# Two small products on opposite halves of TensorE's rows

## The chip, the cores and the metric

The kernel runs on one core of one Trainium2 chip. The metric is the device time of one execution in microseconds (us), the lower the better. The granted clock of TensorE was between 0.997 and 1.000.

## The reference, cut to what matters

```python
# q, k, v: (8 batches, 8 heads, 576 tokens, 64)
q_s = softmax(q, axis=-1)                      # over the 64 of a token
k_s = softmax(k, axis=2)                       # over the tokens
kv  = einsum('bhsd,bhse->bhde', k_s, v)        # K^T V: 64 x 64 for each head
x   = einsum('bhsd,bhde->bhse', q_s, kv)       # x: 576 x 64 for each head
# heads side by side: x is 4608 x 512
out = (silu(x @ w_gate) * (x @ w_val)) @ w_out # widths 512 -> 1536 -> 512
```

Most of the work is the feed-forward part in the last line. This case is about the two einsums, "kv" and "x".

## The kernel before

TensorE is an array of 128 x 128. Both einsums use it as four tiles of 64 x 64: the upper and the lower half of the rows (the contraction), times the left and the right half of the columns (the output partitions). `HALF[0]` and `HALF[1]` are the two halves of the partitions. In kv the row half is `g`, in x it is the head `h`; the other letter is the column half.

```python
    def kv_mm(b, G, kv, c):
        ek = st[b, G]["ek"]
        for t in range(T):                      # T = 9
            for g in range(2):                  # row half
                for h in range(2):              # column half
                    nc.tensor.matmul(
                        out=kv[g][HALF[h], c:c + 65], lhsT=ek[HALF[g], t, h, :],
                        rhs=vbs[G][HALF[g], t, h, :],
                        start=(t == 0), stop=(t == T - 1),
                    )

    def x_and_next_kv(b, with_kv=True):
        # ... 8 PSUM banks: main (4), kv (2), tail (2)
        def quads(o, c, G, t0, t1):
            for g in range(2):                  # column half
                for h in range(2):              # row half
                    nc.tensor.matmul(
                        out=o[h][HALF[g], c:c + 64 * (t1 - t0)], lhsT=kn[HALF[h], g, G, :],
                        rhs=qt[G][HALF[h], t0:t1, 64 * g:64 * g + 64],
                        start=True, stop=True,
                    )

        for G in range(NG):                     # NG = 2 groups of four heads
            quads(main[G], 0, G, 0, 8)          # x of batch b: 4 matmuls of 512 columns
            if more:
                kv_mm(b + 1, G, kv, 256 * G)    # kv of batch b + 1: 36 of 65 columns
        for G in range(NG):
            quads(tail, 64 * G, G, 8, T)        # x, last 64 columns
        # ... ScalarE and VectorE copy the banks out
```

I call one run of the two last loops a block. Every matmul is preceded by a load of its stationary operand (`lhsT`, 64 columns). The feed-forward matmuls `g_ps`, `u_ps`, `o_ps` (128 x 128, up to 512 columns) fill the time between the blocks; the prediction's "m unit" is one pair of `g_ps` and `u_ps` with the work of ScalarE and VectorE (`hr`) on it, and a bank is one of the buffers in PSUM that the matmuls write. Five blocks have x and kv together: x of batches 2 to 6.

The softmax here doesn't subtract the row's maximum and nothing guards it: scores larger than these inputs give would overflow.

## Time and profile before

| | before |
|---|---|
| median of 3 runs | 311.7 us (311.62 to 311.92) |
| span of the profiled run | 309.7 us |
| TensorE busy / VectorE / ScalarE | 302.8 / 161.9 / 146.3 us |
| one block, first x matmul to next g_ps | 1.298 us |
| five blocks | 6.5 us, 2.1% of the time |

How to read it: only TensorE counts, and of TensorE's time the change touches a fiftieth. The profile's lines for this, the waits and the timeline of a block are shown in the prediction. A timeline merges equal instructions; the trace also holds each instruction's start on its own, in whole nanoseconds. Where I give starts in ns they are such single records, counted from the first matmul of the block of batch 3. Matmul ends are modelled by the profile. The starts hardly vary: the five blocks of the kernel before took 1.297 or 1.298 us each.

### The profile page before, as it was taken

Reading aid. Unit: us, or ns where it says so; the run is one execution under the profiler, and the core shown is the slowest. Engines: PE = TensorE matmul, PEld = TensorE weight load, DVE = VectorE, ACT = ScalarE, POOL = GpSimd, SP = SyncE. Lnnn points to the kernel's source line nnn. Section 1 sums busy time; section 2 is a strip of 40 time slices with the busy share of each in tenths; the row PEclk is TensorE's granted clock in tenths of the full one; section 3 lists DMA queues with packets and bytes.
Section 4 is the critical chain, followed back from the end, with each engine's and each line's share of the span. In section 5 each row is a group of like instructions: output and inputs, shape, how many; then the busy total and the mean of one; then the engine's idle time right before and its main releaser. Section 6 shows DMA issues by size and latency. Waiting matters only on the chain.

```text
span 309.7 us, 5467 instructions
## 1 busy us (share of the span) xinstructions
PE 302.8 (98%) x2182; PEld 150.3 (49%) x2182; DVE 161.9 (52%) x286; ACT 146.3 (47%) x214; POOL 32.8 (11%) x39
## 2 busy tenths in 40 slices
PE   6999999999999999999999999999999999999995
PEld 2688745554445444454445444544444444444443
DVE  3844477945754566365826492639353324433421
ACT  5843578785674375547464737455043113312300
POOL 2960021510200110002000200000000000000000
PEclk9999999999999999999999999999999999999999
DMA  7999999999347815590739352605310302020133
GB/s 273 189 195 207 275 389 389 349 219 389 79 87 200 327 33 114 135 382 13 144 74 353 102 121 61 186 0 107 72 35 0 70 11 56 3 68 8 26 71 103
DMA packets 43018, 45.78 MB, mean 148 GB/s; under 512 B 19568, under 2 KB 28272, under 8 KB 42992
## 3 DMA queue, kind: packets, MB, share of 16 engines
q1 hardware_dynamic: 34096, 39.95, 43.4%
q0 software_dynamic: 8752, 5.31, 12.0%
q8 instruction: 17, 0.28, 0.4%
q10 hardware_dynamic: 144, 0.16, 0.2%
q14 instruction: 9, 0.07, 0.1%
HBM read 37.75 MB, written 9.44 MB: 152 GB/s over the span
## 4 chain that ended last, share of the span: by engine, by line
PE 96%; DMA 1%; DVE 0%; ACT 0%; issue 0%
PE g_ps L284 30%; PE u_ps L284 30%; PE o_ps L317 29%; PE kv L189 2%; PE xp L245 1%; PE idle L388 1%; DMA q<-in_q_dram 1%; PE tp L164 1%; PE o_ps L338 1%; DVE rs L135 0%; PE xp L202 0%; PE kv L411 0%; ACT eq L121 0%; ACT xt L259 0%; PE ks L397 0%; DVE o_sb L342 0%
## 5 line engine op out<-in xcount | busy, mean ns | idle before, releaser
L291 ACT ACTIVATE sg<-g_ps 128x512 bf16<-128x512 f32 (+2 forms) x120 | 64.7, 554 | 133.6 <-PE g_ps L284 120.5
L293 DVE TENSOR_TENSOR hr<-sg,u_ps 128x512 bf16<-128x512 bf16 (+3 forms) x120 | 72.5, 616 | 86.3 <-PE u_ps L284 80.7
L284 PE MATMUL g_ps<-xt,wg 128*128 128x512 bf16 (+2 forms) x480 | 111.4, 358 | 0.1
L284 PE MATMUL u_ps<-xt,wv 128*128 128x512 bf16 (+2 forms) x480 | 111.3, 358 | 0.0
L317 PE MATMUL o_ps<-wo,hr 128*128 128x512 bf16 x420 | 93.9, 379 | 0.0
L284 PEld LDWEIGHTS <-wv 128*128 128x128 bf16 x480 | 46.9, 98 | 46.4
L284 PEld LDWEIGHTS <-wg 128*128 128x128 bf16 x480 | 46.3, 98 | 45.5 <-issue 0.6
L317 PEld LDWEIGHTS <-hr 128*128 128x128 bf16 x420 | 40.9, 98 | 48.6
L110 DVE COPY o_sb<-o_ps 128x512 f32<-128x512 f32 x33 | 22.4, 680 | 39.0 <-PE o_ps L317 39.0
L124 POOL CAST vb<-v 128x1152 bf16<-128x1152 f32 x14 | 17.8, 1277 | 135.8 <-DMA v<-in_v_dram 106.6
L135 DVE TENSOR_REDUCE rs<-eq 128x18 f32<-128x1152 bf16 (+2 forms) x18 | 21.7, 1213 | 12.7 <-ACT eq L121 12.7
L149 DVE TENSOR_TENSOR qs<-eq,rr 128x1152 bf16<-128x1152 bf16 (+2 forms) x18 | 22.1, 1234 | 0.1
L121 ACT ACTIVATE eq<-q 128x1152 bf16<-128x1152 f32 (+2 forms) x18 | 18.3, 1051 | 4.1 <-DMA q<-in_q_dram 4.0
L121 ACT ACTIVATE ek<-k 128x1152 bf16<-128x1152 f32 (+2 forms) x17 | 17.9, 1101 | 0.5 <-DMA k<-in_k_dram 0.5
L291 ACT ACT_TABLE_LOAD x12 | 15.4, 1283 | 0.2
L121 ACT ACT_TABLE_LOAD x11 | 14.1, 1283 | 0.2
L388 PE MATMUL idle<-zero 128*128 128x512 bf16 x20 | 7.9, 560 | 2.6 <-DVE rs L135 1.4
L259 ACT CAST xt<-xp 128x512 bf16<-128x512 f32 x14 | 7.8, 586 | 4.5 <-PE xp L245 4.5
L260 DVE CAST xt<-xp 128x512 bf16<-128x512 f32 x14 | 9.0, 683 | 0.7 <-PE xp L245 0.7
L189 PEld LDWEIGHTS <-ek 64*64 64x64 bf16 x504 | 6.3, 107 | 1.7 <-ACT qt L108 0.4
L189 PE MATMUL kv<-vb,ek 64*64 64x65 bf16 x504 | 6.7, 194 | 0.0
L245 PE MATMUL xp<-qt,kn 64*64 64x512 bf16 (+1 forms) x112 | 6.7, 292 | 0.0
(44 smaller groups left out, 67.4 us busy)
## 6 DMA issues: line engine op xcount, KB each, us to landing
q<-in_q_dram SPq DMA_DIRECT2D x16, 576.0 KB, 5.4
out_dram<-o_sb SPq DMA_DIRECT2D x70, 128.0 KB, 2.3
k<-in_k_dram SPq DMA_DIRECT2D x12, 576.0 KB, 7.2
v<-in_v_dram SPq DMA_DIRECT2D x12, 576.0 KB, 9.1
wo<-in_moe_w_out_dram POOLq DMA_DIRECT2D x4, 384.0 KB, 15.4
k<-in_k_dram SPq DMA_DIRECT2D x4, 320.0 KB, 8.2
k<-in_k_dram SPq DMA_DIRECT2D x4, 256.0 KB, 8.1
v<-in_v_dram SPq DMA_DIRECT2D x2, 320.0 KB, 6.9
```

Source lines behind the costliest of these rows:

```text
L110: eng.tensor_copy(out=out, in_=in_)
L121: nc.scalar.activation(out=e[:, t0:t1], in_=src[:, t0:t1], func=AF.Exp)
L124: return nc.gpsimd.tensor_copy(out=vbs[G][:, :, :, 0:64], in_=raw["v", b, G].rearrange("p h (t d) -> p t h d", d=64),)
L135: i = nc.vector.reduce_sum(out=rs[:, 2 * t0:2 * t1], in_=eq2[:, 2 * t0:2 * t1, :], axis=mybir.AxisListType.X)
L149: last = eng.tensor_mul(qs[:, t0:t1, :].rearrange("p t (h d) -> p (t h) d", d=64), eq2[:, 2 * t0:2 * t1, :], s["rr"][:, 2 * t0:2 * t1].to_ ...
L189: nc.tensor.matmul(out=kv[g][HALF[h], c:c + 65], lhsT=ek[HALF[g], t, h, :], rhs=vbs[G][HALF[g], t, h, :], start=(t == 0), stop=(t == T - 1),)
L245: nc.tensor.matmul(out=o[h][HALF[g], c:c + 64 * (t1 - t0)], lhsT=kn[HALF[h], g, G, :], rhs=qt[G][HALF[h], t0:t1, 64 * g:64 * g + 64], star ...
L284: nc.tensor.matmul(out=gu[a][i][:, 0:w_], lhsT=(wg, wv)[a][:, kk, ms], rhs=xt[:, kk, c:c + w_], start=(kk == 0), stop=(kk == KT - 1),)
L291: nc.scalar.activation(out=sg[:, 0:w_], in_=g_ps[:, 0:w_], func=AF.Silu)
L293: nc.vector.tensor_mul(hr[:, m, r:r + w1], sg[:, 0:w1], u_ps[:, 0:w1])
L317: nc.tensor.matmul(out=o_ps, lhsT=hr[:, m, r0:r0 + 128], rhs=wo[:, m, :], start=(m == 0), stop=(m == MT - 1),)
L388: i = nc.tensor.matmul(out=idle, lhsT=zero[:, 0:128], rhs=zero, start=True, stop=True)
```

## The change

While one half of the rows makes x, the other half makes kv of the next batch; then the halves swap. The whole change:

```diff
-    def kv_mm(b, G, kv, c):
+    def kv_mm(b, G, kv, c, halves=(0, 1)):
...
-            for g in range(2):
+            for g in halves:
...
-        def quads(o, c, G, t0, t1):
+        def quads(o, c, G, t0, t1, heads=(0, 1)):
             for g in range(2):
-                for h in range(2):
+                for h in heads:
...
         for G in range(NG):
-            quads(main[G], 0, G, 0, 8)
             if more:
-                kv_mm(b + 1, G, kv, 256 * G)
+                for h in range(2):
+                    quads(main[G], 0, G, 0, 8, (h,))
+                    kv_mm(b + 1, G, kv, 256 * G, (1 - h,))
+            else:
+                quads(main[G], 0, G, 0, 8)
```

The same instructions, in another order. A phase is now 2 x matmuls on one half and 18 kv matmuls (nine steps of two) on the other; a block has four phases and the tails of x.

## The prediction

> **What bounds the kernel now.** I read the page first (busy shares, then the chain that ended last), then the waits of TensorE, then the timeline around one of the blocks that the change touches. The page's first part:
>
> ```profile
> PE 302.8 (98%) x2182; PEld 150.3 (49%) x2182; DVE 161.9 (52%) x286; ACT 146.3 (47%) x214; POOL 32.8 (11%) x39
> PEclk9999999999999999999999999999999999999999
> PE 96%; DMA 1%; DVE 0%; ACT 0%; issue 0%
> ```
>
> TensorE (PE) is busy for 302.8 of the span's 309.7 us and makes 96% of the chain that ended last; the other engines are busy for half the span or less. The clock is at full speed in all slices. A busy PE is not a PE at its peak, but it says that no engine and no transfer is waited for during most of the span. TensorE's list of waits confirms it:
>
> ```profile
> PE idle L388 <- DVE rs L135: 1.4, 1, 1.4
> PE idle L388 <- DVE sel L367: 1.2, 1, 1.2
> PE xp L202 <- DVE kn L424: 0.4, 1, 0.4
> ```
>
> All three waits, 3.0 us together, are in the first stage (batch 0, its own code, not touched). So time is won or lost only by what TensorE itself takes for its instructions in program order. The touched lines are small there:
>
> ```profile
> L189 PE MATMUL kv<-vb,ek 64*64 64x65 bf16 x504 | 6.7, 194 | 0.0
> L245 PE MATMUL xp<-qt,kn 64*64 64x512 bf16 (+1 forms) x112 | 6.7, 292 | 0.0
> ```
>
> Each is 6.7 us busy, and not all of it changes: K^T V (called kv here) of batches 3 to 7 runs inside the x function, that of 1 and 2 elsewhere; x of batches 1 and 7 has no kv with it and keeps its old order. Five blocks change (x of batch 2 with kv of 3, up to x of 6 with kv of 7). TensorE's timeline of one of them:
>
> ```profile
> 98.29 1.03 PE L284 MATMUL u_ps<-xt,wv 128*128 128x512 bf16 x4
> 99.25 0.41 PE L245 MATMUL xp<-qt,kn 64*64 64x512 bf16 x4
> 99.49 0.51 PE L189 MATMUL kv<-vb,ek 64*64 64x65 bf16 x36
> 99.81 0.41 PE L245 MATMUL xp<-qt,kn 64*64 64x512 bf16 x4
> 100.03 0.52 PE L189 MATMUL kv<-vb,ek 64*64 64x65 bf16 x36
> 100.36 0.25 PE L245 MATMUL xp<-qt,kn 64*64 64x64 bf16 x8
> 100.54 1.04 PE L284 MATMUL g_ps<-xt,wg 128*128 128x512 bf16 x4
> ```
>
> Start times are what counts here, since a matmul's length contains its way through the array, in which the next one already streams. The block takes 1.29 us, 99.25 to 100.54: x of four heads 0.24, kv 0.32, x 0.22, kv 0.33, the tails of x (columns 512 to 575) with the drain before the next 128x128 matmuls 0.18. The five blocks have the same figures within 0.01 us. Thus all that the change touches is 5 x 1.29 = 6.5 us, 2% of 311.7.
>
> **What the Trainium skill says.** (1) "TensorE: Matmul & The Clock Gate", "Part 3: Packing small matmuls — row/col tiling": matmuls on different tiles of the array run concurrently, issued some 4 ns apart, a weight load may overlap a running matmul when the row group differs, and matmuls are in program order in start and in end. The trace agrees with the concurrency: the four x matmuls of one group of heads start within 10 ns at 99.25, on the four 64x64 tiles. Whether a short matmul on one half runs beside a long one on the other, no run has shown yet, since the kernel before always gives all four tiles the same work at the same time. (2) Same page, "Back-to-back issue gap": N/2.4 + 2.5 ns. For 512 columns this is 216 ns; the timeline's g_ps and u_ps runs of 4 start 0.86 us apart, 215 ns each. For 65 columns it is 29.6 ns; single records inside the kv runs start in groups of four (one for each tile), 29 to 36 ns apart, mean 32, and the last group of a run comes 53 to 60 ns after the one before. (3) "TensorEngine Tiling (Array Packing)", "Key Properties": a change of tiling mode drains the array. Both orders enter and leave the 64x64 mode once per block, so this cost stays.
>
> **The change part by part.** Nothing is removed or added: the program has as many TensorE instructions as before (2182 matmuls with their loads), with the same shapes, and the order of the built programs on VectorE, ScalarE, GpSimd and SyncE is the same. The changed order is only this, for each of the two groups of heads: before, x on all four tiles (4 matmuls of 512 columns), then kv on all four (9 steps of 4 matmuls, 65 columns). After, x on the upper two tiles (2 matmuls of 512) while kv runs on the lower two (9 steps of 2); then the halves swap.
>
> The work of one tile is the same: one x stream of 213 ns (512/2.4) and nine kv steps. Before, a group of heads takes (0.24 + 0.32 + 0.22 + 0.33)/2 = 0.555 us. After, it takes two phases, each as long as the longer of the two things in it: x, 0.22 to 0.24, or nine kv steps. Now kv is the longer, so x is hidden, but kv's nine steps come twice, one half of the rows each, and the shorter x leaves its half idle until the phase ends. Everything depends on the time of one kv step on two tiles:
> - If it stays at the 32 ns of now, a phase is 8 x 32 + some 40 for the last step and the swap = 0.296, a group 0.59, a block 4 x 0.296 = 1.18 against 1.11: +0.07 us, and five blocks +0.37 us.
> - If it falls to 29 ns, since only 4 instructions (two loads, two matmuls) go to a step in place of 8 (at the end of the runs the single records are some 4.2 ns apart, so 8 of them take 33 ns, which is near the step), a phase is 8 x 29 + 40 = 0.272, a block 1.09: -0.02, five blocks -0.1 us.
> - The floor: one tile's own work, 213 + 9 x 27 = 456 ns for a group (65/2.4 = 27), -0.1 us each against 0.555, ten groups -1.0 us. The change cannot reach it, because x (213) and kv (243) are not equally long.
>
> The 40 ns is my choice between an ordinary step and the 53 measured, since half as many matmuls end there. I give the first case 60%, the second 40%: about +0.2 us.
>
> Off the path: ScalarE evacuates the banks of the first head (h = 0) of each pair, VectorE those of the second. The first head's x comes as early as before, the second's a phase (0.3 us) later. Before, ScalarE began at 99.70, VectorE at 100.03, because it was busy with hr until then; by my sum the second head's x of the first group ends at 99.25 + 0.30 + 0.41 = 99.96, still earlier than VectorE is free. The second bank ends at some 100.54 where VectorE came to it at about 100.65. So evacuation does not move, and the next g_ps and u_ps find their banks as before. A slip of 0.1 us would be hidden too, because VectorE has 1 us of slack in each m unit.
>
> **The rivals.** *No overlap.* If a short matmul may not finish before the long one issued ahead of it, or a tile waits for the other row half, a phase is x plus kv: 0.24 + 0.30 = 0.54, a block 4 x 0.54 = 2.16, +1.05 each, five blocks +5.2 us: 316.9, still under 2%. For it: the page's words on the order of ends. Against: kv matmuls last 190 ns from start to end and x 400, so an order of ends alone would delay only what follows, and in the second group of the block above the tiles leave x one by one, kv's first matmul of each tile starting some 221 ns after that tile's own x, not after the last x. That shows tiles that run on their own. I give it 12%.
>
> *A real gain.* If array and issue overlap better than I think (the loads of the next x hidden under the other half's kv, no 53 ns at the ends), a block could come to 1.0 us and five save up to 0.6 us: 311.1. For it: the ends of the runs cost 20 to 30 ns each now. Against: the imbalance of the phases.
>
> *Evacuation becomes a wait.* If VectorE's later start held back a bank, TensorE would show a wait on DVE in the m unit after a block, at most 0.3 us each, 1.5 us in all. The slack above speaks against it.
>
> **The range and the chances.** Main case 311.7 + 0.2 = 311.9 us. The runs before spread over 0.3 us. With the gain of 0.6 below and partial overlap above (a third of the 5 us), I take 311.0 to 313.4. Even the floor (-1.0) and the rival without overlap (+5.2) lie within 2% (6.2 us): within 97%, faster by over 2% 1%, slower by over 2% 2%.
>
> **What the changed profile would show.** Right: in a block, a kv matmul starts within some 20 ns of x, not 0.24 us later; the four phases start some 0.27 to 0.30 us apart; the block from first x to next g_ps takes 1.25 to 1.37 us; TensorE's list of waits still has the three entries of the first stage alone. The step on two tiles decides between my two cases: 32 or 29 ns. Wrong: kv starts 0.2 us after x in each phase, and a block takes over 2 us (no overlap); or a block under 1.2 us (real gain); or TensorE waits for DVE or ACT after a block; or a lower granted clock, which I exclude from one core at 1.000.

## The result, and the profile after

| | before | after |
|---|---|---|
| median of 6 runs each | 311.69 us (311.61 to 311.92) | 311.69 us (311.33 to 312.3) |
| ratio, 95% interval | | 1.0002 (0.9989 to 1.0015): the same |
| one block | 1.298 us | 1.311 us |
| profile: start to the first of the five blocks | 68.70 us | 69.39 us |
| profile: from there to x of batch 7 | 160.47 us | 160.54 us |
| profile: from there to the end | 80.57 us | 80.53 us |

The middle part, from the first of the five blocks to x of batch 7, is where the change acts, and it is the measure that I use below: in the one kernel that was profiled twice (kv6_first) it repeats to about 0.01 us. It grew by 0.07 us, five times the block's 0.013. The first part is noisy: over thirteen profiled runs it lay between 68.2 and 69.8 us, whatever the kernel. In the profiled run of the changed kernel it shows as a fourth wait in TensorE's list, at the first v, ahead of everything that the change touches:

```profile
PE kv L415 <- DMA v<-in_v_dram: 2.0, 1, 2.0
PE idle L392 <- DVE rs L135: 1.6, 1, 1.6
PE idle L392 <- DVE sel L371: 1.2, 1, 1.2
PE xp L202 <- DVE kn L428: 0.4, 1, 0.4
```

There is no wait in the blocks or after them, and the copies out of the banks did not move: in this block ScalarE starts 0.45 and VectorE 0.78 us after the first x, in both kernels. TensorE's timeline of the same block as in the prediction (start us, length us; lines of the source have moved by 4 below the change):

```profile
98.99 1.03 PE L288 MATMUL u_ps<-xt,wv 128*128 128x512 bf16 x4
99.95 0.40 PE L245 MATMUL xp<-qt,kn 64*64 64x512 bf16 x2
99.96 0.48 PE L189 MATMUL kv<-vb,ek 64*64 64x65 bf16 x22
100.27 0.38 PE L245 MATMUL xp<-qt,kn 64*64 64x512 bf16 x2
100.27 0.44 PE L189 MATMUL kv<-vb,ek 64*64 64x65 bf16 x16
...
100.84 0.38 PE L245 MATMUL xp<-qt,kn 64*64 64x512 bf16 x1
100.84 0.40 PE L189 MATMUL kv<-vb,ek 64*64 64x65 bf16 x13
101.05 0.22 PE L245 MATMUL xp<-qt,kn 64*64 64x64 bf16 x2
101.07 0.20 PE L189 MATMUL kv<-vb,ek 64*64 64x65 bf16 x2
101.09 0.24 PE L245 MATMUL xp<-qt,kn 64*64 64x64 bf16 x6
101.26 1.04 PE L288 MATMUL g_ps<-xt,wg 128*128 128x512 bf16 x4
```

Three things are to be seen.

1. **The overlap is real.** kv starts at 99.96, with x, where before it started 0.24 us after x.
2. **The halves do not keep program order.** Only 18 kv matmuls stand ahead of the second pair of x in the program, yet 22 started before it. Four kv matmuls of the second phase, on the half that x had just left, overtook the x that waited for the other half. Single records: they start at 240 to 288 ns, that x at 315.
3. **There are holes.** Two kv matmuls come every 32 ns on average, but in the middle of the second phase there are gaps. In the block of batch 3 the starts numbered 29 to 36, counted from the block's first matmul in order of time, are:

```
number     29   30   31   32   33   34   35   36
start ns  350  354  383  387  427  462  470  491
```

The 33rd start comes 40 ns after the 32nd, the next after 35 more. The third phase has a smaller hole (693 to 721 to 754 ns); in the fourth I find none.

The number 32 is the lead. 32 matmuls with their loads are 64 instructions, and the first two x matmuls end at 401 and 404 ns, 23 ns before the 33rd start. That suggested a theory for the experiments: TensorE has 64 instructions in hand, they leave in program order, and a long matmul at the head stops the supply until it has left. The third phase fits: its hole starts with the 53rd matmul, 32 behind the x that is the 21st in the program and ends at 693 ns.

### The profile page after: what moved, and what is told of

It reads as the page before. It is cut to its first block, busy times and chain, and to the rows that moved or that the text cites. A ratio compares the mean times of both kernels' runs of the same rounds, so it can differ in the third digit from the quotient of the medians.

```text
span 310.5 us, 5471 instructions
## 1 busy us (share of the span) xinstructions
PE 301.2 (97%) x2182; PEld 150.5 (48%) x2182; DVE 161.7 (52%) x286; ACT 146.7 (47%) x214; POOL 32.6 (11%) x39
## 4 chain that ended last, share of the span: by engine, by line
PE 95%; DMA 3%; DVE 0%; issue 0%; ACT 0%; SPq 0%
PE g_ps L288 30%; PE u_ps L288 30%; PE o_ps L321 29%; PE kv L189 2%; DMA v<-in_v_dram 2%; DMA k<-in_k_dram 2%; PE xp L245 1%; PE o_ps L342 1%; PE tp L164 1%; PE kv L415 0%; PE xp L202 0%; ACT xt L263 0%; SPq L77 0%; DVE o_sb L346 0%; PE ks L401 0%
## 5 line engine op out<-in xcount | busy, mean ns | idle before, releaser
L392 PE MATMUL idle<-zero 128*128 128x512 bf16 x20 | 6.3, 470 | 2.8 <-DVE rs L135 1.6
L245 PE MATMUL xp<-qt,kn 64*64 64x512 bf16 (+1 forms) x112 | 8.3, 290 | 0.0
L189 PE MATMUL kv<-vb,ek 64*64 64x65 bf16 x504 | 8.2, 195 | 0.0
L189 PEld LDWEIGHTS <-ek 64*64 64x64 bf16 x504 | 7.4, 107 | 0.8 <-ACT ek L121 0.4
```

The source lines that it names most:

```text
L189: nc.tensor.matmul(out=kv[g][HALF[h], c:c + 65], lhsT=ek[HALF[g], t, h, :], rhs=vbs[G][HALF[g], t, h, :], start=(t == 0), stop=(t == T - 1),)
L245: nc.tensor.matmul(out=o[h][HALF[g], c:c + 64 * (t1 - t0)], lhsT=kn[HALF[h], g, G, :], rhs=qt[G][HALF[h], t0:t1, 64 * g:64 * g + 64], star ...
```

## The experiments

All variants change only the order inside a block, except x_split, which also cuts each x in two, and two that are wrong. First, four kernels. Theory W is the window of 64 with halves that start on their own; theory P is the prediction's, that matmuls start in program order.

**kv_first: kv ahead of x in each phase.**

```diff
                 for h in range(2):
-                    quads(main[G], 0, G, 0, 8, (h,))
                     kv_mm(b + 1, G, kv, 256 * G, (1 - h,))
+                    quads(main[G], 0, G, 0, 8, (h,))
```

> The changed kernel with kv ahead of x inside each phase, the same instructions. Theory W (window): TensorE has at most 64 loads and matmuls in hand, they leave in program order, and inside these 64 each row half starts its own next matmul without waiting for the other half. Then a 400 ns x matmul at the head holds the window, and with x behind kv the window moves freely: x starts within 0.1 us of kv, no hole of 40 ns in the kv runs, a group of heads 0.50 to 0.53 us, the block (first matmul to next g_ps) 1.13 to 1.22 us in place of 1.31. Theory P (of the prediction: matmuls start in program order, a phase is nine kv steps): x can start only after the last kv of its phase has started, the block is 1.8 us or more. In the whole time W saves 5 x 0.12 = 0.6 us, P costs 2.5 us.

Measured: 314.05 us, ratio 1.0089 (1.0072 to 1.0106), block 1.801 us. Its timeline:

```profile
99.32 0.38 PE L189 MATMUL kv<-vb,ek 64*64 64x65 bf16 x12
99.51 0.40 PE L245 MATMUL xp<-qt,kn 64*64 64x512 bf16 x2
99.53 0.57 PE L189 MATMUL kv<-vb,ek 64*64 64x65 bf16 x18
99.91 0.40 PE L245 MATMUL xp<-qt,kn 64*64 64x512 bf16 x2
```

Theory W as I had stated it falls: x did not start with kv, although it was only 36 instructions behind. Theory P's time came true, but not its mechanism: x started after 12 of its 18 kv, not after all. Each phase now takes 0.40 us: 0.19 until x may start, then x, and the next kv needs the half that x occupies. The time also gives a check: 5 x (1.801 - 1.298) = 2.5 us, and the medians differ by 314.05 - 311.52 = 2.5 (the 0.9% is clear of the noise, though "slower" is said only from 2% on). So the blocks' length accounts for the whole difference.

**same_half: x, then kv on the same half, then the other half.**

```diff
-                    kv_mm(b + 1, G, kv, 256 * G, (1 - h,))
+                    kv_mm(b + 1, G, kv, 256 * G, (h,))
```

> The changed kernel with kv on the same row half as the x before it, then the other half: in program order nothing lies beside x. Theory P (starts in program order): x and kv of one half, then x and kv of the other, a group of heads 1.05 us, a block 2.1 to 2.2 us. Theory W (window of 64, halves start on their own): the second half's x is 40 instructions behind the first's, within 64, so it starts within 0.05 us of it, and the block takes 1.2 to 1.4 us.

Measured: block 1.899 us (one run, 314.93 us).

```profile
100.20 0.40 PE L245 MATMUL xp<-qt,kn 64*64 64x512 bf16 x2
100.44 0.35 PE L189 MATMUL kv<-vb,ek 64*64 64x65 bf16 x12
100.61 0.40 PE L245 MATMUL xp<-qt,kn 64*64 64x512 bf16 x2
```

Both theories miss. Again the other half's x started after 12 of 18 kv.

**half_by_half: one half does both groups (80 instructions), then the other.**

```diff
+        for h in range(2 if more else 0):
+            for G in range(NG):
+                quads(main[G], 0, G, 0, 8, (h,))
+                kv_mm(b + 1, G, kv, 256 * G, (h,))
```

(in place of the loop over `h` inside `G`)

> One row half does x and kv of both groups of heads (80 instructions), then the other half does. Theory W: the second half's x is 80 instructions behind, outside of 64, so it starts only once the first x has left, 0.40 to 0.45 us after the block's start; the block takes 1.45 to 1.9 us. Theory P: the second half starts after the first half's last matmul has started, some 1.05 us after the block's start, block 2.1 us. If the window were larger than 80, the second half would start at once and the block take 1.2 us.

Measured: block 2.096 us (one run, 316.28 us). The first of the five took 2.565: there the second group's x started 972 ns into the block in place of 523, and TensorE's list of waits has an entry for it, a transposed q that came late:

```profile
PE xp L245 <- DMA qt<-qs: 0.3, 1, 0.3
```

The timeline of the second block:

```profile
100.75 0.40 PE L245 MATMUL xp<-qt,kn 64*64 64x512 bf16 x2
101.00 0.45 PE L189 MATMUL kv<-vb,ek 64*64 64x65 bf16 x18
101.28 0.38 PE L245 MATMUL xp<-qt,kn 64*64 64x512 bf16 x2
101.50 0.35 PE L189 MATMUL kv<-vb,ek 64*64 64x65 bf16 x12
101.66 0.40 PE L245 MATMUL xp<-qt,kn 64*64 64x512 bf16 x2
```

The third x (the other half's first) starts at 0.91 us, after 12 of the 18 kv of the group ahead of it. The block is as long as theory P said, but this start fits neither theory. In three orders six matmuls were still waiting when the other half's matmul was let through. So a second limit stands beside the window: a matmul can pass at most about six that wait for the other half.

**before_kv_first: the kernel before, all four tiles alike, with kv ahead of x.**

```diff
         for G in range(NG):
-            quads(main[G], 0, G, 0, 8)
             if more:
                 kv_mm(b + 1, G, kv, 256 * G)
+            quads(main[G], 0, G, 0, 8)
```

> The kernel before with kv ahead of x, all four tiles alike as before. It separates the window from the halves. Theory W: the ends of the kv runs lose their 53 to 60 ns step, because no x matmul sits at the head of the window when kv needs it; block 1.22 to 1.27 us in place of 1.29. Theory P: no change, 1.28 to 1.30.

Measured: block 1.376 us, outside both expectations (one run, 311.42 us; middle part 160.79 us against 160.47). The first kv run, with no x ahead of it, had no hole: in place of 323 ns it took 308 to the next x. The second kv run, behind x, kept a gap of 34 ns before its 32nd matmul, as both runs have in the kernel before. So the late ends of the kv runs belong to the x ahead of them and not to the swap as such. From the first to the last matmul the block was 0.05 us shorter than before. It lost that and more to a thing that I had not thought of: x came 0.3 us later, so its banks were copied out later, and the next g_ps seems to have waited for the first of them: it starts 253 ns after the last x matmul, in place of 125 before. The list of waits does not show this; I read it from the times.

```profile
99.56 1.14 ACT L259 CAST xt<-xp 128x512 bf16<-128x512 f32 x2 [0.90 <-PE xp L245]
99.67 0.47 PE L245 MATMUL xp<-qt,kn 64*64 64x512 bf16 x12
100.20 1.02 PE L284 MATMUL g_ps<-xt,wg 128*128 128x512 bf16 x4
```

ScalarE's two copies take 0.57 us each, so the first ends at about 100.13, and g_ps starts at 100.20; the last x matmul had started at 99.95. That order is paid for outside of TensorE.

From these runs I formed theory L: (a) a look-ahead of about six matmuls past the other half, (b) a window of 64 that a long matmul at its head blocks. It makes a positive prediction: with a few kv, but not more than six, ahead of x, x starts at once and the window reaches further into the next phase. A second set of four tested it.

**kv4_first, kv6_first and kv12_first: 4, 6 or 12 of the 18 kv ahead of x.** `t0` and `t1` limit kv_mm's steps; N is 2, 3 or 6.

```diff
                 for h in range(2):
+                    kv_mm(b + 1, G, kv, 256 * G, (1 - h,), 0, N)
                     quads(main[G], 0, G, 0, 8, (h,))
-                    kv_mm(b + 1, G, kv, 256 * G, (1 - h,))
+                    kv_mm(b + 1, G, kv, 256 * G, (1 - h,), N, T)
```

> The changed kernel with 4 of the 18 kv matmuls of each phase ahead of x, 14 behind it. What the first four runs left standing, theory L: (a) a matmul may start ahead of at most about 6 matmuls that still wait for the other row half, and (b) at most 64 loads and matmuls are in hand and leave in program order, so a 400 ns x matmul stops the supply 64 instructions behind it until it has left. With 4 kv ahead, x starts with the block (within 0.03 us), and 30 matmuls behind x take the work up to the 14th kv of the next phase, which is not due before x has left: no holes of 40 to 50 ns in the kv runs. Block (first matmul to next g_ps) 1.16 to 1.24 us in place of 1.31 (changed) and 1.30 (before); whole time 0.3 to 0.6 us below the kernel before, 311.0 to 311.3. Rival S (the holes are the price of each swap of the halves, not of the window): the holes stay, block 1.28 to 1.33.

> As kv4_first with 6 kv ahead of x, on the edge of what (a) allows. Theory L: x starts within 0.04 us of the block's first matmul, with none or at most 2 kv started before it, block 1.16 to 1.24. If the look-ahead is shorter than 6, x starts one or two kv steps later (0.03 to 0.09 us per phase), block 1.3 to 1.5.

> As kv4_first with 12 kv ahead of x. Theory L (6 may still wait): x starts when 6 of the 12 have started, some 0.09 to 0.11 us after the block's first matmul, and each later phase is delayed alike: block 1.45 to 1.65, between kv4_first and kv_first (1.80). Rival: x starts once a fixed number of 12 has started (in all three earlier runs 12 of 18 had): then x starts only after all 12, 0.2 us after the block's start, and the block takes 1.8.

Measured: blocks of 1.243, 1.225 and 1.434 us. kv4_first: 311.48 us, ratio 0.9992 (0.9971 to 1.0012), the same. Its time missed the expected 311.0 to 311.3; its middle part, 160.19 us, is 0.28 below before's, which is less than the whole times can show. The timelines of kv6_first and of kv12_first, first lines:

```profile
99.57 0.22 PE L189 MATMUL kv<-vb,ek 64*64 64x65 bf16 x2
99.59 0.40 PE L245 MATMUL xp<-qt,kn 64*64 64x512 bf16 x2
99.62 0.43 PE L189 MATMUL kv<-vb,ek 64*64 64x65 bf16 x20
99.87 0.38 PE L245 MATMUL xp<-qt,kn 64*64 64x512 bf16 x2
```

```profile
99.18 0.28 PE L189 MATMUL kv<-vb,ek 64*64 64x65 bf16 x6
99.28 0.40 PE L245 MATMUL xp<-qt,kn 64*64 64x512 bf16 x2
99.30 0.48 PE L189 MATMUL kv<-vb,ek 64*64 64x65 bf16 x18
```

With 12 ahead x starts after exactly 6, with 18 ahead after 12: so six may wait; it is not a fixed number that must have started. (With 12 the block came out a little better than my 1.45 to 1.65.) With 6 ahead x starts 0.02 us into the block, and the second phase's x 0.30 us into it. The block is 0.086 us shorter than the changed kernel's and 0.073 shorter than before's. Rival S, that every swap of halves costs a hole, falls: kv4_first swaps as often, and the starts numbered 31 to 36 in its block lie at 380, 383, 409, 413, 444, 448 ns, in step.

**x_split: each x of 512 columns as two of 256, one behind the other, in the changed kernel's order.**

```diff
-                    quads(main[G], 0, G, 0, 8, (h,))
+                    for t0 in (0, 4):
+                        quads(main[G], 64 * t0, G, t0, t0 + 4, (h,))
```

> The changed kernel with each x of 512 columns as two matmuls of 256, one right behind the other, in the old order. Theory L: the second piece ends as late as the whole did and stands in the same place, so it stops the supply as long, and there are 16 more instructions in a block: holes stay, block 1.30 to 1.38. Rival M (what hurts is the long single matmul itself): the holes vanish, block 1.2.

Measured: block 1.380 us, on the upper edge of theory L. A shorter matmul alone, in the same place, does not help; I did not run the pieces apart. The single records also test the count. The first two pieces end at 293 and 297 ns and so leave early; the window then reaches to the 34th matmul of the program. By 389 ns the 34th has started (with two x pieces ahead of it still waiting for their half), and the 35th starts at 429, 26 ns after the second pieces' first end at 403.

**kv_narrow and kv_thin: what sets the 32 ns of a kv step?** Both are the changed kernel with wrong results: in the seven middle steps of kv, 33 moving columns in place of 65 (kv_narrow), then also 48 stationary columns in place of 64 (kv_thin).

```diff
-                        out=kv[g][HALF[h], c:c + 65], lhsT=ek[HALF[g], t, h, :],
-                        rhs=vbs[G][HALF[g], t, h, :],
+                        out=kv[g][HALF[h], c:c + (w := 65 if t in (0, T - 1) else 33)],
+                        lhsT=ek[HALF[g], t, h, :], rhs=vbs[G][HALF[g], t, h, 0:w],
```

> The changed kernel with 33 moving columns in place of 65 in the seven middle steps of every kv (its result is wrong on purpose). It asks what sets the kv step of some 32 ns. If it is the stream of columns, the step falls to 20 ns or less, both on two tiles (blocks) and on four (the two kv runs that stand alone, where the supply of 4.2 ns per instruction allows no less than 33 ns for 8). If it is the load of 64 weight columns that stands ahead of every matmul of a tile, the step stays at 27 to 32 ns on two tiles, and the blocks stay at 1.25 to 1.31 us. I expect the load: 27 to 32 ns.

> kv_narrow (33 moving columns in the seven middle steps, its blocks and its step of 32 ns were those of the changed kernel) with 48 stationary columns in place of 64 in the same steps (wrong on purpose). If the load of the stationary operand sets the step, it falls on two tiles to some 24 ns (32 x 48/64) and a phase of the block's first group gets shorter by about 7 x 8 = 56 ns, as far as x (0.24 us) lets it; block 1.10 to 1.25 us. If the step is a fixed cost of a load and a matmul on the same tile, it stays at 32 and the block at 1.31.

Measured: kv_narrow has blocks of 1.312 us and a step of 32 ns, the changed kernel's numbers. Half the stream made no difference. kv_thin has a step of 25 ns on two tiles, and blocks of 1.284. So the load of the stationary operand sets the step: a quarter fewer of its columns, 7 ns less. The records of the loads agree: on a tile, a load starts 1 to 3 ns after the matmul before it, and its own matmul on average 30 ns later with 64 columns and 24 with 48. My block for kv_thin (1.10 to 1.25) was too low, because I had left the window out of that sum. The starts show it, and make the best evidence for the window:

| | first two x end, ns | 32nd start | 33rd start | gap |
|---|---|---|---|---|
| changed kernel | 401, 404 | 387 | 427 | 40 |
| kv_narrow | 400, 403 | 381 | 427 | 46 |
| kv_thin | 400, 403 | 354 | 427 | 73 |

However fast the kv steps are, the 33rd matmul starts at 427 ns, 23 to 24 ns after x has ended. What kv gains, the hole takes. A plain limit on unfinished matmuls is no rival: at the 32nd start only 20 of the 32 are unfinished by the records. What fits is the distance to the oldest: the first load has ended, and the 64 instructions from the first x matmul to the 33rd load have all been issued. In the kernel before, theory L alone does not give the hole: the gap of 34 ns comes after 35 starts, and the 36th start is 94 ns after the last of the four x has ended.

**kv6_timed: kv6_first again, five rounds.**

> kv6_first again, timed against the kernel before in five rounds. By its trace it saves 5 x 0.072 = 0.36 us, 0.12%: ratio 0.9985 to 0.9995, and an interval of some 0.15% either way will hardly separate it from 1. If the ratio is below 0.997 or above 1.001, the blocks' lengths are not what sets the whole time.

Measured: 311.27 us against 311.43, ratio 0.9995 (0.9982 to 1.0007): the same. The profile's middle part is 160.11 us (160.10 in the run before) against 160.47 before and 160.54 changed, so the 0.36 us are there; the start of the kernel varies by more. By the runs alone neither kernel is beaten.

## Why the prediction was right

The time, the class and the range were right: 311.69 measured, 311.9 predicted, 311.0 to 313.4. But the interval of the ratio is 0.4 us to either side, so the time alone could not have told the prediction's two cases apart; the blocks do. Step by step:

- **Bound.** Right. TensorE alone sets the time; the waits of the first stage stayed the only ones, with one more there.
- **Overlap, and the rival without it.** kv runs beside x (99.95 and 99.96), so the rival of 316.9 us falls.
- **The step on two tiles.** The first case was right: 32 ns, not 29. kv_thin shows why: it is the load. The formula in the prediction's point (2) counts the streamed columns alone; its 29.6 ns for 65 columns lies near the 32 by chance, since 33 columns left the step at 32. The thought behind the second case, the supply of instructions, was wrong for two tiles. On four tiles the supply is near: kv_thin's first kv run that stands alone, with all four, has steps of 25 ns at first and mostly of 33 later.
- **The sum of a block.** The size was right by luck (1.18 for four phases plus 0.18 is 1.36, or 1.27 in the second case; measured 1.311), but from two errors that cancel. First, "each as long as the longer of the two things in it" is wrong: the half that has finished x does not wait for the swap but goes on with its kv, by 75 ns in the second phase. Second, the holes of 40 to 75 ns were not in the sum at all; I had seen the 53 to 60 ns at the ends of the kv runs before, and taken them for the price of a swap; before_kv_first shows that a run without x ahead of it ends without one. With kv6_first's 1.225 us as the block without holes, the first error is worth some 0.135 us and the holes 0.086 (estimates: kv6_first also moves x). As a result five blocks cost 0.07 us, between the +0.37 and the -0.1 that I gave.
- **"A real gain".** That was there to be had: -0.36 us in the middle part with kv6_first, of the 0.6 that I called the most. It needed an order of instructions that fits both limits; the imbalance that I held against it did not stop it, because the half that is free first goes on.
- **Evacuation.** Right for the changed kernel: no wait. In before_kv_first, where the first head's x is late, it did become a wait.

So where did the expected gain go? Running x beside kv hides x, but doubles the kv steps in a block from 18 to 36, and a step costs 32 ns on two tiles as on four. What was left, the head start of the free half, went into the holes. kv6_first takes the holes away and so wins 0.36 us, too little for the whole times to show.

What stays open: that instructions leave in program order is concluded from the 33rd start and the end of x, whose ends the profile models; no run shows the queue itself, nor what sets the six of the look-ahead. The holes of the kernel before are tied to x, but not explained in their place.

## What to carry to other kernels

Before giving two halves of an array different work, ask what a step costs on half the tiles; if a load sets it, splitting the work in space doubles the number of steps, and the gain is only what lies beside. Place a long matmul so that few short ones wait ahead of it (here at most six), and so that the 64 instructions from it on last until it has ended. When an effect is a thousandth of the time, measure the stretch of the trace that it acts on, not the whole.

## What the Trainium skill lacked or had wrong

- "TensorE: Matmul & The Clock Gate", "Part 3: Packing small matmuls — row/col tiling" says that matmuls keep program order in start and end. Here four kv matmuls on one row half started at 240 to 288 ns, ahead of an x on the other half that stands before them in the program and started at 315; and by the records a kv that started at 7 ns ended at 221, the x ahead of it at 401.
- The same page, "Part 1: The HAM clock gate (the "warmup" mystery)", gives TensorE a queue of 64 with partial reordering. It does not say that a long matmul at its head holds up the supply: the 33rd matmul of a block started at 427 ns in three kernels whose 32nd started at 354, 381 and 387, with the second x ending at 403 or 404.
- No page has how far one row half may run ahead of the other: six matmuls waited in each of kv_first, same_half, half_by_half and kv12_first.
- The same page, "LDWEIGHTS (loading the stationary operand)", gives columns / 1.2 in ns; an estimate by it is 53 ns for 64 columns and 40 for 48. On 64 x 64 tiles a whole step of load and matmul on one tile took 32 ns with 64 columns and 25 with 48.
